# A fused attention and expert kernel: values and next scores of a tile issued together, in halves of one lasting PSUM pair

## The chip, the cores and the metric

The kernel runs on one core of a Trainium2 chip. The metric is the device time of one execution in microseconds (us). Before the change three runs took 1549.22, 1547.12 and 1549.45 us; their median is 1549.22 us. The engines are TensorE (PE, with its weight loads as PEld), VectorE (DVE), ScalarE (ACT), GpSimd (POOL) and the queue that issues the transfers (SP).

## The reference

The input is q, k and v for 8 batches of 8 heads, 576 positions and 64 channels. Attention is local: each chunk of 64 positions attends to itself only. Its output, as 4608 tokens of 512 channels, goes through four experts with a hidden width of 1024, and every token sums all four with normalised probabilities.

```python
scores = scale * np.matmul(q_c, k_c.transpose(0, 1, 2, 4, 3))   # chunks of 64
scores = scores - np.max(scores, axis=-1, keepdims=True)
attn = np.exp(scores)
attn = attn / (np.sum(attn, axis=-1, keepdims=True) + 1e-09)
out = np.matmul(attn, v_c)
...
p = domain_probs / (domain_probs.sum(-1, keepdims=True) + 1e-09)
for e in range(E):
    h = np.maximum(x @ w1[e], 0.0)
    out += p[:, e:e + 1] * (h @ w2[e])
```

## The kernel before

**Tiles and passes.** A tile is 128 tokens with all eight heads, so two chunks. Four tiles make a subset of 512 tokens, two subsets make a pair. The first subset is done plainly in eight passes over the experts' halves (0 to 7); then come four pairs of eight passes each. A product with float32 precision is made of three matmuls on a high and a low part (`hi` is a rounded copy by ACT, `lo` a subtraction by POOL or DVE). In the pairs the products go through a seven-product scheme for 2 by 2 blocks: `g` and `h` are the two column groups of the first layer (methods `p1` to `p7` of `Group`), `a` and `b` those of the second layer (`Outer`). Pair 0 holds sums and differences made in `first_pair_pass`, the later pairs run `later_pass`, where the second layer of one pass is woven with the first layer of the next by the list `WOVEN`, 28 products of six matmuls each. `first_later_pass` (list `FIRST`) starts that weave, `last_products` (list `ALONE`) ends it.

**Attention of a later tile.** The 32 tiles of the four pairs are prepared while earlier products run, one tile after the other: `a_scores` (16 matmuls of 64 by 64), `a_softmax` (maximum and subtraction on DVE, exponential on ACT), `a_weights` (sum, reciprocal and product on DVE), `a_transpose` (four PE transposes, and a copy by ACT), `a_values` (16 matmuls of 64 by 64, and a copy by ACT into `xraw`). All five use tiles of the PSUM pool `ps_a`, whose one buffer `psa` is a pair of banks: scores take it, transposes take it again, and values a third time. Between them stand products. For the tiles of pairs 0 and 1 the object `Beside` issues one step whenever its rate says so; for the tiles of pairs 2 and 3 the table `TILES` names for each pass which tile takes the places `EARLY` (4, 6, 9, 11) or `LATE` (13, 17, 21, 24) of the 28.

**PSUM and order.** Six further banks, A0 to C1, hold the products' results. The kernel is written with a manual schedule: each engine does its instructions in the order in which the functions issue them, and an instruction waits for those of other engines that used the same tile before it.

**Start and end.** `startup` fills PE with idle matmuls (`keep_warm`, 12, 14 and 3 of them) while the loads and the softmax of the first two tiles run. The idle matmuls write one bank of a `psa` pair, and the row sums of the first softmax (`start_weights`) stand in the other bank of that same pair. At the end `last_products` turns the last pair's result by PE transposes, tile by tile, and stores it.

**The joint of two pairs.** In the last pass of a pair the differences of the next pair's tokens (class `Tokens`, `t1` to `t4`) are made and split. The low part of `t4` is made by POOL in the next pair's first pass, between the splits of the hidden values (L268 in the trace).

Of the kernel before, what the change touches and what calls it, by code (L numbers as in the profile page):

```python
# [15 lines left out]
P = 128  # L16
C = 64
# [7 lines left out]
WAITS = {"loads": 12, "softmax": 14, "copy": 3}  # L25
# [5 lines left out]
def chunk_attention_moe(ctx: ExitStack, tc: tile.TileContext, qk, v, v0, dp, w1, w2, out):  # L31
# [64 lines left out]
    def transpose_probs():  # L96
        flat = by_e[0].rearrange("p e t -> p (e t)")
        for i in range(0, p_rows, P):
            n = min(P, p_rows - i)
            psa = bank()[:n, :P]  # L100
            rows = hpool.tile([P, P], F32, name="s3")[:n]
            nc.tensor.transpose(psa, flat[:, i : i + n], ident)
            nc.scalar.copy(out=rows, in_=psa)
            nc.sync.dma_start(out=p_t[i : i + n, :], in_=rows)
# [6 lines left out]
    xraw = {}  # L111

# [35 lines left out]
    def a_weights(t):  # L148

        s = st[t]  # L150
        s["e"] = att.tile([P, HG, 2, C], F32, name="e")
        z = s["psa"][:, 0, HG * C : HG * C + 2 * HG].rearrange("p (c j) -> p c j", c=2)
        a_norm(s["e"].rearrange("p j c k -> p c j k"), s["sc"], z)

    def a_transpose(t):
        s = st[t]
        ps = ps_a.tile([P, 2, 2 * HG * C], F32, name="psa")[:, 0].rearrange("p (j q) -> p j q", q=P)
# [39 lines left out]
    STEPS = (a_scores, a_softmax, a_weights, a_transpose, a_values)  # L197

    def attention(pair, together):
# [571 lines left out]
    def outputs(pair, i, g):  # L771

        psa = ps_a.tile([P, 2, 2 * HG * C], F32, name="psa")[:, 0].rearrange(
            "p (i m d) -> p i m d", i=2, d=P
        )
        for j in range(2):
            for m in range(2):
                output_part(pair, i + j, g + 2 * m, psa[:, j, m])
        stage = att.tile([P, 2, 2, P], F32, name=("e", "pt")[i // 2 % 2])
        nc.scalar.copy(out=stage, in_=psa)  # L780
# [71 lines left out]
    idle = ps_a.tile([P, 2, SUB], F32, name="psa")  # L852

    def keep_warm(n, cols=SUB):

        for _ in range(n):
            nc.tensor.matmul(
                idle[:, 0, :cols], lhsT=zeros[:, :P], rhs=zeros[:, :cols], start=True, stop=True
# [18 lines left out]
    def start_weights(t):  # L877
        es[t] = att.tile([P, 2 * HG, C], F32, name=("e", "pt")[t % 2])
        a_norm(es[t], sc[t], idle[:, 1, t * 2 * HG : (t + 1) * 2 * HG])

    def startup(beside):
# [11 lines left out]
        for f, k in QUADS[:2]:  # L893
# [48 lines left out]
    class Beside:  # L942


        def __init__(self, pair, n):
            self.steps = attention(pair, pair == 0) if pair < n_pairs else iter(())
            self.rate, self.due = len(STEPS) * PAIR * NT / n, 0.0

# [171 lines left out]
    EARLY, LATE = (4, 6, 9, 11), (13, 17, 21, 24)  # L1120
# [20 lines left out]
    def first_later_pass(n, *_):  # L1141
# [27 lines left out]
    def later_pass(n, ahead, late):  # L1169
# [13 lines left out]
        second_half(at, ahead[0], ahead[2:])  # L1183
# [15 lines left out]
        if n % 2 and more:  # L1199
            add(at, 5, lambda: probs_load(n + 1, 0))  # L1200
# [4 lines left out]
        late, x_low = [], []  # L1205
# [4 lines left out]
        if last_pass and more:  # L1210
# [18 lines left out]
        return (sc, left, *x_low), late  # L1229

    def second_half(at, sc, x_low=()):
# [6 lines left out]
        add(at, 4, *x_low, lambda: sc.sum("t4", 1, nc.gpsimd))  # L1238
        add(at, 6, lambda: sc.hi("t4", 1), lambda: sc.lo("t4", 1))

    def last_products(ahead):
# [4 lines left out]
        psa = []  # L1246

        def places(names):
            both = ps_a.tile([P, 2, 2 * HG * C], F32, name="psa")
            for t in (both[:, 0], both[:, 1], *(bank(name) for name in names)):  # L1250
                psa.append(t.rearrange("p (m d) -> p m d", d=P))

        def parts(i, *ms):
            for m in ms:
                output_part(pair, i, m, psa[(i + NT) % (2 * NT)][:, m])

        def store(i, eng):
# [88 lines left out]
```

## Time and profile before

| | |
|---|---|
| median of 3 runs | 1549.22 us (1547.12 to 1549.45) |
| the profiled execution's own time | 1546.54 us |
| its span | 1544.8 us |
| PE busy | 1524.5 us (99%) |
| PEld busy | 1239.6 us (80%) |
| DVE busy | 915.7 us (59%) |
| POOL busy | 888.5 us (58%) |
| ACT busy | 574.8 us (37%) |
| transfers | 314.16 MB, 203 GB/s on average |

The time of an execution holds the span and 1.7 us around it. PE is occupied in nearly the whole span, so a change is worth what it takes from, or adds to, the time between two of PE's products. In the tables of the profile a line number is that of the kernel before; L455 is the helper that issues all products, L139 the scores, L168 the values, L175 the copy of the values, L517 the copy of a running sum.

### The profile page before, as it was taken

To read this page: it belongs to the slowest core of one execution; us is meant where nothing else is said; L and a number is where in the kernel's file an instruction comes from. 1 tells how busy PE (TensorE), PEld (TensorE's weight loads), DVE (VectorE), ACT (ScalarE), POOL (GpSimd) and SP (SyncE) were. 2 spreads that over 40 slices of the span, in tenths; PEclk is the share of its full clock that TensorE was granted. 3 is DMA by queue.
4 is the path that set the end of the run, shared out by engine and by line. 5 is a ranking of instruction groups with operands and counts; after the bars stand their busy time and mean duration, and the time that the engine had idled before them with its cause. 6 is when DMAs were issued, how large, how long until landed. Compare 5 with 4: busy or idle time off the path is not lost.

```text
span 1544.8 us, 23430 instructions
## 1 busy us (share of the span) xinstructions
PE 1524.5 (99%) x8863; PEld 1239.6 (80%) x8863; DVE 915.7 (59%) x1284; ACT 574.8 (37%) x1000; POOL 888.5 (58%) x668
## 2 busy tenths in 40 slices
PE   8999999999999999999999999999999999999998
PEld 6878877888888887888888778888888788888886
DVE  4444454444443456677676855666767746666665
ACT  3343443444443434333333444333333343333332
POOL 2343577776666716555556855555557656555554
PEclk9999999999999999999999999999999999999999
DMA  5434348977676676666666667676666676666663
GB/s 193 123 122 148 101 134 278 312 248 226 234 245 205 208 268 205 200 224 215 208 207 198 201 211 227 200 226 208 223 189 198 189 234 198 200 201 203 201 191 135
DMA packets 164832, 314.16 MB, mean 203 GB/s; under 512 B 14177, under 2 KB 79985, under 8 KB 164721
## 3 DMA queue, kind: packets, MB, share of 16 engines
q1 hardware_dynamic: 164720, 312.68, 62.8%
q8 instruction: 70, 1.15, 0.3%
q14 instruction: 42, 0.34, 0.1%
HBM read 244.39 MB, written 68.23 MB: 202 GB/s over the span
## 4 chain that ended last, share of the span: by engine, by line
PE 78%; POOL 3%; DVE 2%; ACT 1%; issue 1%; DMA 0%; DVEq 0%; SPq 0%; POOLq 0%; ACTq 0%
PE A L455 41%; PE C L455 22%; PE B L455 12%; POOL hfl L637 2%; PE psa L168 1%; PE psa L139 1%; DVE xl L268 1%; PE psa L159 1%; PE psa L769 1%; DVE acc L683 1%; POOL wraw L628 0%; POOL xl L268 0%; DVE wraw L628 0%; ACT hfh L634 0%; ACT xh L265 0%
## 5 line engine op out<-in xcount | busy, mean ns | idle before, releaser
L637 POOL TENSOR_TENSOR hfl<-wraw,hfh 128x512 fp32r<-128x512 f32 x288 | 386.1, 1360 | 207.6 <-ACT hfh L634 205.7
L455 PE MATMUL A<-xh,wf 128*128 128x512 f32 (+1 forms) x1112 | 382.4, 390 | 3.9 <-ACT s L517 3.7
L455 PE MATMUL A<-hfh,wf 128*128 128x512 f32 x768 | 271.2, 394 | 1.6 <-DVE acc L683 1.0
L634 ACT CAST hfh<-wraw 128x512 fp32r<-128x512 f32 x288 | 174.2, 623 | 217.6 <-POOL wraw L628 57.5
L455 PEld LDWEIGHTS A<-xh,wf 128*128 128x128 f32 x1112 | 207.8, 188 | 49.8 <-ACT s L517 5.5
L517 ACT COPY s<-A 128x512 f32<-128x512 f32 x192 | 112.7, 587 | 347.2 <-PE A L455 343.0
L455 PE MATMUL A<-xl,wf 128*128 128x512 f32 (+1 forms) x556 | 214.8, 387 | 0.0
L455 PE MATMUL C<-xh,wf 128*128 128x512 f32 (+1 forms) x584 | 201.1, 391 | 0.0
L455 PEld LDWEIGHTS A<-hfh,wf 128*128 128x128 f32 x768 | 144.2, 188 | 33.1 <-DVE acc L683 2.5
L683 DVE TENSOR_TENSOR acc<-A,acc 128x512 f32<-128x512 f32 x174 | 119.3, 686 | 77.3 <-PE A L455 76.4
L455 PE MATMUL A<-hfl,wf 128*128 128x512 f32 x384 | 149.7, 390 | 0.0
L455 PE MATMUL C<-hfh,wf 128*128 128x512 f32 x384 | 135.4, 394 | 0.2
L268 POOL TENSOR_TENSOR hfl<-wraw,hfh 128x512 fp32r<-128x512 f32 x64 | 86.0, 1371 | 83.4 <-ACT hfh L265 79.8
L455 PEld LDWEIGHTS C<-xh,wf 128*128 128x128 f32 x584 | 109.1, 188 | 23.2
L455 PE MATMUL B<-xh,wf 128*128 128x512 f32 (+1 forms) x384 | 126.9, 383 | 0.0
L268 POOL TENSOR_TENSOR wf<-wraw,wf 128x512 fp32r<-128x512 f32 x70 | 91.4, 1331 | 55.9 <-ACT wf L265 53.6
L455 PEld LDWEIGHTS A<-xl,wf 128*128 128x128 f32 x556 | 104.3, 188 | 20.7
L628 POOL TENSOR_TENSOR wf<-wraw,wf 128x512 f32<-128x512 f32 x23 | 29.8, 1294 | 156.3 <-DVE wf L622 156.3
L455 PE MATMUL C<-xl,wf 128*128 128x512 f32 (+1 forms) x292 | 112.8, 388 | 0.0
L683 DVE TENSOR_TENSOR acc<-C,acc 128x512 f32<-128x512 f32 x90 | 62.1, 691 | 60.7 <-PE C L455 54.8
L637 POOL TENSOR_TENSOR hfl<-wf,hfh 128x512 fp32r<-128x512 f32 x48 | 71.2, 1483 | 35.5 <-ACT hfh L634 35.5
L455 PEld LDWEIGHTS C<-hfh,wf 128*128 128x128 f32 x384 | 72.1, 188 | 16.3 <-DVE acc L683 1.1
(175 smaller groups left out, 2735.5 us busy)
## 6 DMA issues: line engine op xcount, KB each, us to landing
wf<-w SPq DMA_DIRECT2D x336, 512.0 KB, 4.1
wraw<-in_w SPq DMA_DIRECT2D x128, 256.0 KB, 3.7
w<-wf SPq DMA_DIRECT2D x112, 256.0 KB, 4.4
qk_in<-in_qk SPq DMA_DIRECT2D x32, 512.0 KB, 4.7
v_in<-in_v SPq DMA_DIRECT2D x32, 256.0 KB, 4.8
w<-hfl SPq DMA_DIRECT2D x32, 256.0 KB, 2.4
w<-hfh SPq DMA_DIRECT2D x32, 256.0 KB, 2.6
w<-hfh SPq DMA_DIRECT2D x48, 128.0 KB, 2.5
```

Of the source, the lines that this page charges most:

```text
L139: nc.tensor.matmul(s["sc"][half, c, j], lhsT=s["x"][rows, g, 0, h], rhs=s["x"][rows, g, 1, h], start=True, stop=True,)
L159: nc.tensor.transpose(ps[:, j], s["e"][:, j].rearrange("p c k -> p (c k)"), ident)
L168: nc.tensor.matmul(av[half, c, j], lhsT=s["v"][rows, 2 * j + odd], rhs=s["pt"][rows, j, half], start=True, stop=True,)
L268: eng.tensor_tensor(out=t[1], in0=src, in1=t[0].bitcast(F32), op=ALU.subtract)
L455: nc.tensor.matmul(out, lhsT=lhs(k, a), rhs=rhs(k, b), start=first and i == 0, stop=last and i == len(parts) - 1, skip_group_check=not (fi ...
L517: nc.scalar.copy(out=t, in_=self.a)
L628: (eng or nc.vector).tensor_tensor(out=self.values[place, k], in0=self.values[a, k], in1=self.values[b, k], op=op)
L634: nc.scalar.copy(out=self.part(name, 0)[:, k], in_=self.values[name, k])
L637: (eng or nc.gpsimd).tensor_tensor(out=self.part(name, 1)[:, k], in0=self.values[name, k], in1=self.part(name, 0)[:, k].bitcast(F32), op=A ...
L683: nc.vector.tensor_tensor(out=acc[key], in0=src, in1=acc[key], op=ALU.add)
L769: nc.tensor.transpose(out_ps, acc[pair + 1, m + NK * s][:, j * P : (j + 1) * P], ident)
```

## The change

1. **One lasting pair.** `psa` is allocated once, and no longer per step. Scores use the first half of the columns of both its banks (`blocks(0)`), values the second half (`blocks(1)`). Transposes still take one whole bank.
2. **Joint steps.** `a_next(t, after)` issues the values of tile t with their copy and, right behind, the scores of the next tile, with the loads for it. The maximum and exponential come one place later. `EARLY` and `LATE` become three places each; for `Beside` a tile has four yields and `rest`, an empty one for pair 0.
3. **Startup.** 10 idle matmuls in place of the first 12; they write bank C1, and the row sums stay in `psa`. The third split of the first weights stands ahead of the first transpose, values of tile 0 ahead of the transposes of tile 1, scores of tile 2 behind these.
4. **Joints of pairs and of stages.** The low part of `t4` goes from POOL to DVE, that of `b22` three places later. In `first_later_pass` the two groups change their banks (index 1 - g), and the split of `t1` and the sum `t4` move behind the split of `b21`. One of the loads of probabilities moves from place 5 to place 13.
5. **Last outputs.** A unit is now one 128-channel plane of four tiles (`plane`): four transposes, one copy (ACT or DVE; the last one is divided between both), one store with rows of 512 bytes. Two planes stand behind b2, five behind a4, one behind b4; before it were two tiles behind b2, four halves and two tiles behind a4, and four halves behind b4.

```diff
-WAITS = {"loads": 12, "softmax": 14, "copy": 3}
+WAITS = {"loads": 10, "softmax": 14, "copy": 3}
...
+    psa = ps_a.tile([P, 2, 2 * HG * C], F32, name="psa")
...
-    def halves(ps):
-
-        return ps[:, :, : HG * C].rearrange("p c (j k) -> p c j k", k=C)
+    def blocks(i):
+
+        return psa[:, :, i * HG * C : (i + 1) * HG * C].rearrange("p c (j k) -> p c j k", k=C)
 
     def a_scores(t):
         s = st[t]
-        s["psa"] = ps_a.tile([P, 2, 2 * HG * C], F32, name="psa")
-        s["sc"] = halves(s["psa"])
+        s["sc"] = blocks(0)
...
-        av = halves(ps_a.tile([P, 2, 2 * HG * C], F32, name="psa"))
+        av = blocks(1)
...
         a_load(first)
+        yield
+        a_next(None, first)
         for t in range(first, last):
-            for step in STEPS:
-                if not (together and step is a_softmax):
-                    yield
-                if together and step is a_transpose:
-                    yield
-                step(t)
-                if step is a_scores:
-                    a_load_v(t)
-                    if t + 1 < last:
-                        a_load(t + 1)
+            for step in (a_softmax, a_weights, *(rest * [None]), a_transpose):
+                yield
+                if step:
+                    step(t)
+            yield
+            a_next(t, t + 1 if t + 1 < last else None)
+
+    def a_next(t, after):
+
+        if t is not None:
+            a_values(t)
+        if after is not None:
+            a_scores(after)
+            a_load_v(after)
+            if (after + 1 - NT) % (PAIR * NT):
+                a_load(after + 1)
...
-            self.names = (*((f"A{g}", f"B{g}", f"C{g}") if apart else ("A0", "B0", "C0")), f"B{g if apart else 0}", "s2")
+            i = 1 - g if apart else 0
+            self.names = (f"A{i}", f"B{i}", f"C{i}", f"B{i}", "s2")
...
-    idle = ps_a.tile([P, 2, SUB], F32, name="psa")
+    idle = bank("C1")
...
-        a_norm(es[t], sc[t], idle[:, 1, t * 2 * HG : (t + 1) * 2 * HG])
+        a_norm(es[t], sc[t], psa[:, 1, t * 2 * HG : (t + 1) * 2 * HG])
...
-        for f, k in QUADS[:2]:
+        for f, k in QUADS[:3]:
             w1_split(f, k, nc.gpsimd)
         start_transpose(0)
         keep_warm(WAITS["copy"])
         start_weights(1)
-        for f, k in QUADS[2:]:
-            w1_split(f, k, nc.gpsimd)
-        start_transpose(1)
         start_values(0)
         start_x(0)
+        start_transpose(1)
+        start_scores(2)
+        w1_split(1, 1, nc.gpsimd)
         start_values(1)
         start_x(1)
-        start_scores(2)
         start_scores(3)
...
-    EARLY, LATE = (4, 6, 9, 11), (13, 17, 21, 24)
+    EARLY, LATE = (6, 9, 11), (17, 21, 24)
...
-        add(at, places[0], lambda: a_scores(t), lambda: a_softmax(t), lambda: a_load_v(t))
-        if i + 1 < PAIR * NT:
-            add(at, places[0], lambda: a_load(t + 1))
-        for place, step in zip(places[1:], STEPS[2:]):
-            add(at, place, lambda step=step: step(t))
+        after = t + 1 if i + 1 < PAIR * NT else None
+        if i == 0:
+            add(at, 13, lambda: a_next(None, t))
+            add(at, 14, lambda: a_softmax(t))
+        add(at, places[0], lambda: a_weights(t))
+        add(at, places[1], lambda: a_transpose(t))
+        add(at, places[2], lambda: a_next(t, after))
+        if after:
+            add(at, places[2] + 1, lambda: a_softmax(after))
...
         put(12, "b22", 1)
-        put(12, "t1", 0)
-        add(at, 12, lambda: sc.sum("t4", 0, nc.gpsimd))
         put(13, "b21", 1)
+        put(13, "t1", 0)
         put(13, "t3", 0)
+        add(at, 13, lambda: sc.sum("t4", 0, nc.gpsimd))
...
-            add(at, 5, lambda: probs_load(n + 1, 0))
+            add(at, 13, lambda: probs_load(n + 1, 0))
...
-            x_low = [lambda: x.lo("t4", nc.gpsimd)]
             late = [
-                (0, lambda: x.hi("b22")), (0, lambda: first_load(pair + 2)), (5, lambda: x.lo("b22")),
+                (0, lambda: x.hi("b22")), (0, lambda: first_load(pair + 2)), (5, lambda: x.lo("t4")),
+                (8, lambda: x.lo("b22")),
             ]
...
+        def plane(s, m, ps, engs):
+
+            ps = ps.rearrange("p (i d) -> p i d", d=P)
+            for j in range(NT):
+                output_part(pair, s * NT + j, m, ps[:, j])
+            pool, name, bufs = stages.pop()
+            stage = pool.tile([P, NT, P], F32, name=name, bufs=bufs)
+            for k, eng in enumerate(engs):
+                part = slice(k * NT // len(engs), (k + 1) * NT // len(engs))
+                eng(out=stage[:, part], in_=ps[:, part])
+            t = (1 + pair * PAIR + s) * NT
+            nc.sync.dma_start(
+                out=out[t * P : (t + NT) * P, m * P : (m + 1) * P].rearrange("(i p) d -> p i d", p=P),
+                in_=stage,
+            )
...
             if name == "b2":
-                places(("C1", "C0"))
-                parts(4, *range(NK))
-                parts(5, *range(NK))
+                plane(1, 0, bank("C1"), act)
+                plane(1, 1, bank("C0"), act)
             elif name == "a4":
...
+                plane(1, 2, psa[:, 0], act)
+                plane(1, 3, bank("B1"), dve)
+                plane(0, 0, bank("B0"), act)
+                plane(0, 1, bank("C1"), dve)
+                plane(0, 2, bank("C0"), act)
...
+        plane(0, 3, bank("A1"), act + dve)
```

**How the instructions move.** On PE, in a later pass, around the values of a tile (`psa<-pt,v_in`) and the scores (`psa<-qk_in`); names of product banks begin with A, B or C, and a row names in brackets the engines or transfers whose count its first matmul waits for. Before, scores of this tile, a product, and much later its values:

```order
L139 MATMUL psa<-qk_in 64x64 [waits DMAHW2_49,PE_49]
L139 MATMUL psa<-qk_in 64x64 x15
L455 MATMUL C_7051<-hfh_6898,wf_6876 128x512 [waits DMAHW7_49]
...
L168 MATMUL psa<-pt,v_in 64x64 [waits DMAHW6_49,Activation_49]
L168 MATMUL psa<-pt,v_in 64x64 x15
L455 MATMUL C_7059<-xh_5522,wf_7008 128x512 [waits DMAHW5_49,DVE_49]
```

The same place in the changed kernel:

```order
L462 MATMUL A_6939<-xh_5519,wf_6923 128x512
L169 MATMUL psa<-pt,v_in 64x64 [waits DMAHW1_49,Activation_49]
L169 MATMUL psa<-pt,v_in 64x64 x15
L140 MATMUL psa<-qk_in 64x64 [waits DMAHW2_49,Activation_49]
L140 MATMUL psa<-qk_in 64x64 x15
L462 MATMUL C_6997<-xh_5473,wf_6971 128x512 [waits DMAHW7_49,DVE_49]
```

The scores of the next tile stand directly behind the values; both rows have a wait for a count of ACT. On ACT the rows of such a place in the changed kernel are these (`pt` is the copy of the transposes, `xraw` that of the values, the row behind it the exponential of the next scores):

```order
L524 COPY s_7397<-A_7299 128x512 [waits PE_49,Activation_49]
L162 COPY pt<-psa 128x512 [waits DVE_49,PE_49]
L176 COPY xraw<-psa 128x2x4x64 [waits PE_49]
L188 ACTIVATE psa<-psa 128x2x256 [waits DVE_49,PE_49,Activation_49]
```

In the program the values wait for the count that the copy into `pt` reaches, and in each of the 28 joints the scores wait for the count that the copy into `xraw` reaches, the copy of the values just ahead of them; before, one or more products stood between that copy and the next scores.

On POOL, at the joint of two pairs, before:

```order
L637 TENSOR_TENSOR hfl_8375<-wf_8252,hfh_8373 128x512 [waits Activation_49]
L268 TENSOR_TENSOR xl_8438<-xraw,xh_8437 128x1024 [waits PE_49]
L628 TENSOR_TENSOR wraw<-wraw 128x512
L637 TENSOR_TENSOR hfl_8480<-wraw,hfh_8478 128x512 [waits Activation_49]
```

and in the changed kernel:

```order
L644 TENSOR_TENSOR hfl_8302<-wf_8178,hfh_8300 128x512 [waits Activation_49]
L635 TENSOR_TENSOR wraw<-wraw 128x512
L644 TENSOR_TENSOR hfl_8407<-wraw,hfh_8405 128x512 [waits Activation_49]
```

The row of 1024 elements (`xl`, the low part of `t4`) has left POOL; it stands on DVE, ahead of the low part of `b22`.

More of the change, by code (lines that the diff above doesn't have):

```diff
@@ L99, in transpose_probs @@
             n = min(P, p_rows - i)
-            psa = bank()[:n, :P]
+            ps = bank()[:n, :P]
             rows = hpool.tile([P, P], F32, name="s3")[:n]
-            nc.tensor.transpose(psa, flat[:, i : i + n], ident)
-            nc.scalar.copy(out=rows, in_=psa)
+            nc.tensor.transpose(ps, flat[:, i : i + n], ident)
+            nc.scalar.copy(out=rows, in_=ps)
             nc.sync.dma_start(out=p_t[i : i + n, :], in_=rows)
@@ L151, in a_weights @@
         s["e"] = att.tile([P, HG, 2, C], F32, name="e")
-        z = s["psa"][:, 0, HG * C : HG * C + 2 * HG].rearrange("p (c j) -> p c j", c=2)
+        z = psa[:, 0, HG * C : HG * C + 2 * HG].rearrange("p (c j) -> p c j", c=2)
         a_norm(s["e"].rearrange("p j c k -> p c j k"), s["sc"], z)
@@ L156, in a_transpose @@
         s = st[t]
-        ps = ps_a.tile([P, 2, 2 * HG * C], F32, name="psa")[:, 0].rearrange("p (j q) -> p j q", q=P)
+        ps = psa[:, 0].rearrange("p (j q) -> p j q", q=P)
         for j in range(HG):
@@ L195, in a_norm, with attention @@
         nc.vector.tensor_tensor(out=e, in0=a, in1=r, op=ALU.mult)
-    STEPS = (a_scores, a_softmax, a_weights, a_transpose, a_values)
-    def attention(pair, together):
+    def attention(pair, rest):
         first = (1 + pair * PAIR) * NT
@@ L771, in outputs @@
     def outputs(pair, i, g):
-        psa = ps_a.tile([P, 2, 2 * HG * C], F32, name="psa")[:, 0].rearrange(
-            "p (i m d) -> p i m d", i=2, d=P
-        )
+        ps = psa[:, 0].rearrange("p (i m d) -> p i m d", i=2, d=P)
         for j in range(2):
             for m in range(2):
-                output_part(pair, i + j, g + 2 * m, psa[:, j, m])
+                output_part(pair, i + j, g + 2 * m, ps[:, j, m])
         stage = att.tile([P, 2, 2, P], F32, name=("e", "pt")[i // 2 % 2])
-        nc.scalar.copy(out=stage, in_=psa)
+        nc.scalar.copy(out=stage, in_=ps)
         t = (1 + pair * PAIR) * NT + i
@@ L857, in keep_warm @@
             nc.tensor.matmul(
-                idle[:, 0, :cols], lhsT=zeros[:, :P], rhs=zeros[:, :cols], start=True, stop=True
+                idle[:, :cols], lhsT=zeros[:, :P], rhs=zeros[:, :cols], start=True, stop=True
             )
@@ L942, in chunk_attention_moe, with __init__ @@
     class Beside:
-        def __init__(self, pair, n):
-            self.steps = attention(pair, pair == 0) if pair < n_pairs else iter(())
-            self.rate, self.due = len(STEPS) * PAIR * NT / n, 0.0
+        def __init__(self, pair, n, rest):
+            self.steps = attention(pair, rest)
+            self.rate, self.due = ((4 + rest) * PAIR * NT + 1) / n, 0.5
         def load(self):
@@ L1182, in later_pass @@
             add(at, i, f)
-        second_half(at, ahead[0], ahead[2:])
+        second_half(at, ahead[0])
         add(at, 12, lambda: sc.sum("t3", 0, nc.gpsimd))
@@ L1204, in later_pass @@
                 attend(at, pair + 1, places, i)
-        late, x_low = [], []
+        late = []
         if first_pass and pair > 1:
@@ L1228, in later_pass, with second_half @@
                 f()
-        return (sc, left, *x_low), late
-    def second_half(at, sc, x_low=()):
+        return (sc, left), late
+    def second_half(at, sc):
         add(at, 0, lambda: sc.sum("t2", 1))
@@ L1237, in second_half @@
         add(at, 4, lambda: sc.hi("t3", 1), lambda: sc.lo("t3", 1))
-        add(at, 4, *x_low, lambda: sc.sum("t4", 1, nc.gpsimd))
+        add(at, 4, lambda: sc.sum("t4", 1, nc.gpsimd))
         add(at, 6, lambda: sc.hi("t4", 1), lambda: sc.lo("t4", 1))
@@ L1245, in last_products @@
         steps = {"ab"[g]: Outer(g, n_run - 1, ahead[1], ahead[0], True) for g in range(2)}
[L1246 to L1257, printed above, removed]
-            name, k = (("s1", 0), ("s2", 0), ("s3", 0), ("wraw", 0), ("wraw", 0), ("wraw", 0), ("e", 0), ("pt", 0))[i]
-            pool = {"e": att, "pt": att, "wraw": wpool}.get(name, hpool)
-            stage = pool.tile([P, SUB], F32, name=name, bufs=N_RAW if name == "wraw" else 1)
-            eng(out=stage, in_=psa[(i + NT) % (2 * NT)].rearrange("p m d -> p (m d)"))
-            t = (1 + pair * PAIR) * NT + i
-            nc.sync.dma_start(out=out[t * P : (t + 1) * P, :], in_=stage)
+        stages = [(hpool, f"s{i}", 1) for i in (1, 2, 3)]
+        stages += [(wpool, "wraw", N_RAW)] * 3 + [(att, "e", 1), (att, "pt", 1)]
+        def plane(s, m, ps, engs):
[12 more added lines that the diff above has]
+            )
+        act, dve = [nc.scalar.copy], [nc.vector.tensor_copy]
         for i, name in enumerate(ALONE):
@@ L1269, in last_products @@
             if name == "b2":
[L1270 to L1272 removed]
+                plane(1, 0, bank("C1"), act)
+                plane(1, 1, bank("C0"), act)
             elif name == "a4":
[L1274 to L1285 removed]
+                plane(1, 2, psa[:, 0], act)
[4 more added lines that the diff above has]
+        plane(0, 3, bank("A1"), act + dve)
     with tc.manual_schedule():
[L1288 removed]
+        beside = [Beside(0, (n_pass - 3) * 2 * NK, 1), Beside(1, (n_pass - 1) * 26 - 4, 0)]
         startup(beside[0])
```

13 lines of the change are left out of this document (removed).

## The prediction

> **What bounds the kernel now.** I read the totals of the page first, then its chain of waits.
>
> ```profile
> span 1544.8 us, 23430 instructions
> PE 1524.5 (99%) x8863; PEld 1239.6 (80%) x8863; DVE 915.7 (59%) x1284; ACT 574.8 (37%) x1000; POOL 888.5 (58%) x668
> PE 78%; POOL 3%; DVE 2%; ACT 1%; issue 1%; DMA 0%; DVEq 0%; SPq 0%; POOLq 0%; ACTq 0%
> ```
>
> PE is occupied in 1524.5 of 1544.8 us, so all that PE ever stands idle is 20.3 us. No transfer appears in the chain. Each part of the change is therefore worth what it takes from, or adds to, the time from one product's start to the next. What PE does in a joint was read from its timeline; L455 is a product, L139 scores, L168 values, L175 their copy.
>
> ```profile
> 1099.55 0.69 PE L168 MATMUL psa<-pt,v_in 64*64 64x64 f32 x32
> 1100.31 0.59 ACT L175 COPY xraw<-psa 128x512 f32<-128x512 f32 x1 [2.73 <-PE psa L168]
> ...
> 1102.80 0.39 PE L455 MATMUL A<-hfh,wf 128*128 128x512 f32 x1
> ...
> 1103.12 0.69 PE L139 MATMUL psa<-qk_in 64*64 64x64 f32 x32
> ...
> 1103.74 0.50 PE L455 MATMUL A<-xh,wf 128*128 128x512 f32 x1
> ...
> 1105.24 0.39 PE L455 MATMUL B<-xh,wf 128*128 128x512 f32 x1
> ...
> 1106.60 0.39 PE L455 MATMUL A<-hfh,wf 128*128 128x512 f32 x1
> ```
>
> A product's six matmuls take 1106.60 - 1105.24 = 1.36 us, 0.23 each. A step set between products costs more than its own streaming: 0.32 from the last product's start to the step's (1103.12 - 1102.80), 0.62 until the next product, less the 0.23 that would pass anyway, and 0.14 because the six matmuls behind it take 1.50 (1105.24 - 1103.74). That is 0.85 per step, 1.71 for values and scores apart.
>
> **Joint steps.** One of the two entries is saved, if the scores follow the values at once. They don't, I think. Both are halves of one tile and of the same two banks, the program orders accesses by tile and not by column, and in the changed program the first score matmul of each of the 28 joints waits for the count that the copy of the values just ahead reaches. The profile of before shows that sharing a pair is enough to wait:
>
> ```profile
> 8.90 3.19 PE L857 MATMUL psa<-s 128*128 128x512 bf16 x14
> ...
> 12.21 0.70 DVE L190 TENSOR_REDUCE psa<-A 128x8 f32<-128x512 f32 x1 [1.65 <-PE psa L857]
> ...
>   ACT xraw L175: 0.4, 1
> ```
>
> The row sums go to one bank of the pair and waited 1.65 us for idle matmuls that fill the other; the last row, from the view of the scores' line, shows one score that stood behind a copy of values already. The Trainium skill ("PSUM — Partial Sum Buffer", section on bank collisions) asks for the same: PSUM is to be guarded by bank and quadrant and not by address, because TensorE writing columns of a bank while another engine reads other columns of it is an error. Under it the scores cannot overtake the copy in halves of a bank; without it the joint would be the first rival below.
>
> The price: the copy ends 1100.31 + 0.59 - 1099.55 = 1.35 us after the values' start. PE restarts about 0.05 after a copy that it awaits (890.73 + 0.58 = 891.31 against 891.36, quoted further down). The joint then takes 0.32 + 1.35 + 0.05 + 0.62 - 0.23 + 0.14 = 2.25, against 1.71: **+0.54, times 28 = +15.2 us**. Behind the waiting score matmul stand all products; nothing else can run on PE.
>
> ACT works in order, and a copy that finds a cast ahead of it ends later:
>
> ```profile
> 706.99 0.69 PE L168 MATMUL psa<-pt,v_in 64*64 64x64 f32 x32
> ...
> 707.09 1.34 ACT L634 CAST hfh<-wraw 128x512 fp32r<-128x512 f32 x2 [0.25 <-PE B L455]
> ...
> 708.34 0.58 ACT L175 COPY xraw<-psa 128x512 f32<-128x512 f32 x1
> ...
>   PE psa L168: 48.1, 18
> ```
>
> Here it ends at 708.92, 1.93 after the values' start, 0.58 later than above. Today nobody waits for that; in a joint PE does. This is the place of a `LATE` tile, and I give 0.58 to each of the six joints at such places: 3.5. The last row, from the view of L175, says that 18 of the 32 copies began on PE's release, so 14 did not; eight of those lie outside `LATE`. I take five of them at 0.58, 2.9. Bounds: none of the late ones (0), or the six at 0.58 and the eight at twice that, as casts also await transfers there (3.5 + 9.3 = 12.8). **Joints: 15.2 + 6.4 = +21.6 us, between +15.2 and +28.0.**
>
> The maximum and exponential one place later, and three places for four, cost nothing: from scores to transposes lie two or more products of 1.36 us and more, DVE is busy 59% and ACT 37%. The loads for the next tile move along with the scores on SP, whose transfers appear nowhere in the chain; the load of probabilities, moved eight places, likewise.
>
> **Joints of pairs.** The low part of `t4` leaves POOL.
>
> ```profile
> 884.37 2.31 DVE L268 TENSOR_TENSOR xl<-xraw,xh 128x1024 fp32r<-128x1024 f32 x1
> ...
> 885.53 3.40 POOL L268 TENSOR_TENSOR xl<-xraw,xh 128x1024 fp32r<-128x1024 f32 x1
> ...
> 888.89 1.28 POOL L628 TENSOR_TENSOR wraw<-wraw 128x512 f32<-128x512 f32 x1
> ...
> 889.50 0.39 PE L455 MATMUL A<-hfh,wf 128*128 128x512 f32 x1
> 890.20 0.62 ACT L634 CAST hfh<-wraw 128x512 fp32r<-128x512 f32 x1 [6.62 <-POOL wraw L628]
> 890.73 0.58 ACT L517 COPY s<-A 128x512 f32<-128x512 f32 x1
> ...
> 891.36 0.50 PE L455 MATMUL A<-xh,wf 128*128 128x512 f32 x1 [1.47 <-ACT s L517]
> ...
> 1221.04 0.50 PE L455 MATMUL A<-xh,wf 128*128 128x512 f32 x1 [1.45 <-ACT s L517]
> ```
>
> POOL's 3.40 us hold the sum, the sum holds ACT's cast, the cast holds the copy of A for which PE stands: 891.36 - 889.50 - 0.23 = 1.63 us. Without it the sum can begin 3.4 earlier and the whole stall goes. On DVE the operation takes 2.31 (row 884.37), and `b22`'s, which stood there, goes three places on, so DVE's load at this place stays. Two such joints: **-3.3 us**; bounds 0 (DVE's sums come late in turn) and -3.8 (with the slow restart of 0.11 and more each).
>
> **First later pass.** PE stands twice where the banks of one group are taken again:
>
> ```profile
> 587.08 0.50 PE L455 MATMUL A<-hfh,wf 128*128 128x512 f32 x1 [0.61 <-DVE wraw L622]
> ...
> 590.48 1.72 POOL L637 TENSOR_TENSOR hfl<-wraw,hfh 128x512 fp32r<-128x512 f32 x1
> ...
> 592.25 0.50 PE L455 MATMUL B<-hfl,wf 128*128 128x512 f32 x1 [1.24 <-POOL hfl L637]
> ```
>
> The exchange of banks takes the first wait away (0.6). The second is POOL's work, and POOL stays back to back there; with the first wait gone PE arrives earlier at it, or at the split of `t1` that is now POOL's later. **-0.9 us**, between 0 and -1.9 plus restarts, -3.
>
> **Startup.** Up to the first products PE's work hangs on DVE's softmax of the first tiles; the row sums' wait is quoted above (12.21).
>
> ```profile
> 17.64 1.09 PE L826 MATMUL B<-ident,pt 128*128 128x128 f32 x4 [2.13 <-DVE pt L195]
> 18.66 1.97 PE L839 MATMUL B<-s,qk_in 64*64 64x64 f32 x32
> 20.42 1.15 PE L839 MATMUL A<-s,qk_in 64*64 64x64 f32 x32
> ...
> 22.84 0.68 DVE L182 TENSOR_REDUCE m<-C 128x8 f32<-128x512 f32 x1
> 23.36 1.21 PE L455 MATMUL B<-xh,wf 128*128 128x256 f32 x8
> ...
> 28.07 0.66 PE L826 MATMUL B<-ident,e 128*128 128x128 f32 x4
> ...
> 10.00:20.00 10.00, 5.74 (x47) 3.52 (x46) 4.11 (x9) 3.83 (x7) 4.97 (x4) 0.86 0.89 314
> ...
> PEld A L815 <- DMA xraw<-in_qk: 0.2, 1, 0.2
> ```
>
> With the idle matmuls in their own bank the row sums lose the 1.65 above, and the second ones a like wait behind the three idle matmuls (estimated as 1.5, since the sums run one behind the other and shift together). In the 10 to 20 us window the granted clock is 0.86, and groups of one kind show it: transposes 1.09 against 0.66 later, values 1.97 against 1.15. If PE gets there earlier, 0.43 + 0.82 of that may go. Together 4.4; but the next softmax's maximum (22.84) needs DVE, which still splits the first tokens, and I give back 0.7: **-3.7 us**, from -1.65 (the first wait alone) to -4.4. Two idle matmuls fewer at the very start bring nothing: of the waits up to 9 us the last row says that the second tile's scores stood for their load after all twelve, and would stand for it longer. Moving the third split of weights costs nothing: POOL does the four in the same order, and is idle 42% of the time.
>
> **Last outputs.**
>
> ```profile
> 1537.40 0.69 DVE L683 TENSOR_TENSOR acc<-A,acc 128x512 f32<-128x512 f32 x1 [2.44 <-PE A L455]
> ...
> 1538.52 0.59 ACT L1261 COPY s<-psa 128x512 f32<-128x512 f32 x1 [2.73 <-PE psa L769]
> ...
> 1540.31 0.68 DVE L1261 COPY wraw<-B 128x512 f32<-128x512 f32 x1
> ...
> 1541.32 0.40 SPq L1263 DMA_DIRECT2D out<-wraw  x1
> ```
>
> After the last sum (ends 1538.09) come four copies and four stores; the last is issued 3.2 us later and lands at the span's end, 3.5 us on. With one plane, behind the sum come 0.43 until a copy could begin (1538.52 - 1538.09), an estimated 0.3 more for four transposes in place of one, 0.4 for half a copy (0.59 undivided, and a part that doesn't shrink), and 0.33 from the last copy's end to the issue (1541.32 - 1540.99): 1.5, so 1.7 sooner, plus up to 0.2 for transfers that no longer queue. Four more transposes ahead of b4 cost some 0.4 (four take 0.66 at 28.07, the last one's drain within). **-1.5 us**, from 0 (rows of 512 bytes land later) to -2.5.
>
> **Sum.** +21.6 - 3.3 - 0.9 - 3.7 - 1.5 = +12.2, on the profiled execution's 1546.54: 1558.7. That execution lies 2.7 below the median of the runs, 1549.22, so for the median 1561.
>
> **Rivals.**
> *The scores don't wait* (the wait is for an older copy, or one that is done). PE then streams 32 more matmuls in one group, 0.69 - 0.22 = 0.47, and a joint takes 0.85 + 0.47 = 1.32 against 1.71: -0.39 times 28 = -10.9. With the other gains -20.3, so 1529. It decides once the pause in a joint is under 0.39 + 9.4/28, some 0.7 us beyond streaming, where the wait is worth 0.93. For it speaks that the columns are disjoint; against it the row sums' 1.65. Chance 6%.
> *The gains eat the loss.* The copies are all on time (+15.2) and startup, pair joints and tail bring their bounds (-4.4 - 3.8 - 3 - 2.5 = -13.7): +1.5, 1551. For it speaks that ACT is idle 63% of the time; against it that 14 copies were late. Chance 10%.
> *ACT blocks.* ACT takes casts that await a transfer or POOL, in order, and the copy stands behind them while PE, standing, makes nothing that would release them: two more us in six joints, +12, so 1573. For it speaks the chance of casts of weights next to the copies in pairs 0 and 1; against it that transfers are no part of the chain. Chance 8%.
> The forecast holds the remaining 76%.
>
> **How the numbers follow.** A measurement of this kernel tells about 0.2%, 3.1 us, from no change. From the sum's bounds: 15.2 - 13.7 to 28.0 - 2 about the median is 1551 to 1575, both corners unlikely together; the range is 1551 to 1570. Faster: the first rival and a little of the second, 8%. Within 0.2%: half of the second and some of the forecast's edge, 7%. Slower: 85%.
>
> **What would show it.** In the changed profile PE's scores should carry an idle time put down to ACT's `xraw` copy, about 28 times near 0.9 us, and PE's busy share should fall. The stalls of 1.47 and 1.45 should be gone, the first product of 256 columns should stand near 19.5, and one copied plane near the end. If the scores start right behind the values, my central step is wrong, and the time is under 1535; if the idle times at joints reach 2 us and more, ACT's order is to blame.

## The result, and the profile after

The changed kernel took 1561.35 us (median of 6 runs, 1559.73 to 1562.41) against 1548.33 us for the kernel before on the same chips (6 runs, 1545.49 to 1549.45): a ratio of 1.0086, 95% interval 1.0073 to 1.0099. It is slower, by 13 us; the forecast was 1561 us, in a range of 1551 to 1570.

The totals of the changed kernel, and the three longest groups of PE's waits, who waited for whom: us in total, times, the longest.

```profile
span 1557.9 us, 23373 instructions
PE 1518.0 (97%) x8861; PEld 1241.3 (80%) x8861; DVE 917.6 (59%) x1287; ACT 572.5 (37%) x1000; POOL 886.2 (57%) x666
...
PE psa L140 <- ACT xraw L176: 25.8, 28, 1.6
PE A L821 <- DMA xraw<-in_qk: 1.7, 1, 1.7
PE C L462 <- POOL hfl L644: 1.5, 2, 1.3
```

PE is busy 6.5 us less than before (1524.5), and the span is 13.1 us longer. One group of waits stands out: the scores (L140 in the changed kernel) behind the copy of the values (L176), once in each of the 28 joints, 25.8 us in all. In a timeline the first two numbers of a row are its start and its length, and brackets hold the idle time before it and who ended it. The first of the two timelines is a joint in which ACT was free, the second one at a `LATE` place.

```profile
1073.35 0.69 PE L169 MATMUL psa<-pt,v_in 64*64 64x64 f32 x32
...
1074.12 0.59 ACT L176 COPY xraw<-psa 128x512 f32<-128x512 f32 x1 [2.79 <-PE psa L169]
...
1074.75 0.69 PE L140 MATMUL psa<-qk_in 64*64 64x64 f32 x32 [0.70 <-ACT xraw L176]
...
1075.38 0.50 PE L462 MATMUL C<-xh,wf 128*128 128x512 f32 x1
```

```profile
716.15 0.69 PE L169 MATMUL psa<-pt,v_in 64*64 64x64 f32 x32
...
716.26 1.34 ACT L641 CAST hfh<-wraw 128x512 fp32r<-128x512 f32 x2 [0.25 <-PE B L462]
...
717.51 0.58 ACT L176 COPY xraw<-psa 128x512 f32<-128x512 f32 x1
...
718.14 0.69 PE L140 MATMUL psa<-qk_in 64*64 64x64 f32 x32 [1.29 <-ACT xraw L176]
```

The scores start 0.04 to 0.05 us after the copy ends (1074.71 and 718.09): 1.40 us after the values' start in the one, 1.99 in the other. No score overtakes a copy, though they use other columns.

### The profile page after: what moved, and what is told of

It is laid out like the page before. It is cut to its first block, busy times and chain, and to the rows that moved or that the text cites. A ratio compares the mean times of both kernels' runs of the same rounds, so it can differ in the third digit from the quotient of the medians.

```text
span 1557.9 us, 23373 instructions
## 1 busy us (share of the span) xinstructions
PE 1518.0 (97%) x8861; PEld 1241.3 (80%) x8861; DVE 917.6 (59%) x1287; ACT 572.5 (37%) x1000; POOL 886.2 (57%) x666
## 4 chain that ended last, share of the span: by engine, by line
PE 89%; DVE 4%; ACT 2%; POOL 2%; DMA 2%; issue 1%; SPq 0%; POOLq 0%; DVEq 0%; ACTq 0%
PE A L462 44%; PE C L462 26%; PE B L462 14%; PE psa L140 1%; ACT xraw L176 1%; PE psa L169 1%; PE psa L160 1%; DVE xl L275 1%; DVE wraw L635 1%; DVE acc L691 1%; ACT hfh L641 1%; POOL wf L275 0%; PE psa L777 0%; DMA w<-wf 0%; DVE wraw L629 0%
## 5 line engine op out<-in xcount | busy, mean ns | idle before, releaser
L462 PE MATMUL A<-xh,wf 128*128 128x512 f32 (+1 forms) x1112 | 380.7, 389 | 1.0 <-ACT s L524 0.7
L462 PE MATMUL A<-hfh,wf 128*128 128x512 f32 x768 | 271.2, 394 | 1.0 <-DVE acc L691 1.0
L462 PEld LDWEIGHTS A<-xh,wf 128*128 128x128 f32 x1112 | 207.8, 188 | 45.6 <-ACT s L524 1.7
L462 PE MATMUL A<-xl,wf 128*128 128x512 f32 (+1 forms) x556 | 214.7, 387 | 0.0
L462 PE MATMUL C<-xh,wf 128*128 128x512 f32 (+1 forms) x584 | 201.0, 391 | 0.0
L462 PEld LDWEIGHTS A<-hfh,wf 128*128 128x128 f32 x768 | 144.2, 188 | 32.4 <-DVE acc L691 2.5
L462 PE MATMUL A<-hfl,wf 128*128 128x512 f32 x384 | 149.7, 390 | 0.0
L462 PE MATMUL C<-hfh,wf 128*128 128x512 f32 x384 | 134.2, 391 | 0.2
L462 PEld LDWEIGHTS C<-xh,wf 128*128 128x128 f32 x584 | 109.1, 188 | 23.0
L462 PE MATMUL B<-xh,wf 128*128 128x512 f32 (+1 forms) x384 | 126.0, 382 | 0.0
L462 PEld LDWEIGHTS A<-xl,wf 128*128 128x128 f32 x556 | 104.3, 188 | 21.1
L462 PE MATMUL C<-xl,wf 128*128 128x512 f32 (+1 forms) x292 | 112.8, 388 | 0.0
L462 PEld LDWEIGHTS C<-hfh,wf 128*128 128x128 f32 x384 | 72.1, 188 | 15.9 <-DVE acc L691 1.1
```

What stands on the lines that cost most here:

```text
L462: nc.tensor.matmul(out, lhsT=lhs(k, a), rhs=rhs(k, b), start=first and i == 0, stop=last and i == len(parts) - 1, skip_group_check=not (fi ...
```

## The experiments

All runs stand beside runs of the kernel before on the same chip; "before" is its median there. Kernels are compared with each other by their ratios to it. Line numbers are each kernel's own: runs made from the changed kernel have products at L462 to L465 and scores at L140, those made from the kernel before at L455 and L139, apart from the joints alone (L462, L140).

**Scores first.** In the joint, the two groups change places:

```diff
     def a_next(t, after):
+        if after is not None:
+            a_scores(after)
         if t is not None:
             a_values(t)
         if after is not None:
-            a_scores(after)
             a_load_v(after)
```

> The changed kernel with one edit: in the 28 joints the next tile's scores are issued first and the values behind them, so that no score stands behind the copy of the values. Theory (the pause is the wait for that copy): the 28 pauses of 25.8 us in total vanish, a joint takes 0.32 + 0.47 + 0.62 - 0.23 + 0.14 = 1.32 us beyond the regular pace instead of the 2.25 to 3.1 measured (69.8 us over all 28), so 28 x 1.32 = 37.0 and the time falls by 32.8 us to about 1528.5. Rival A (a group of 64 small matmuls, or the turn from values to scores, is slow by itself): the pause stays, 1561. Rival B (PE gets ahead, and waits for DVE or ACT on the same pair of banks elsewhere): between 1535 and 1555, with new waits at transposes or values.

Measured: 1526.64 us against 1547.71, ratio 0.9865 (0.9852 to 0.9879), so 2.2% or 34 us under the changed kernel. A joint of it by PE's timeline:

```profile
716.93 0.39 PE L463 MATMUL A<-xh,wf 128*128 128x512 f32 x1
717.25 0.69 PE L140 MATMUL psa<-qk_in 64*64 64x64 f32 x32
717.77 0.65 PE L169 MATMUL psa<-pt,v_in 64*64 64x64 f32 x32
718.34 0.50 PE L463 MATMUL C<-xh,wf 128*128 128x512 f32 x1
```

From product to product it takes 1.41 us, in 27 of the 28 joints; less the regular 0.23 and with 0.14 for the restart it is 1.32, the price that I had written for a joint without the wait. Over all 28 joints the start times of PE's matmuls give 37.0 us beyond the regular pace in this kernel, 69.2 in the changed one, and 47.7 for 56 separate steps (0.852 each, from the 64 of before). So the idea of a shared entry is worth its 10.7 us, and the wait took 32.2 back. Rival A falls: values and scores in one group cost nothing by themselves. Rival B too: no wait at values or transposes took its place. This kernel is faster than both.

**The joint undone.** Values at their place, the scores of the next tile one product later; the lasting pair and all else as changed.

```diff
-        add(at, places[2], lambda: a_next(t, after))
+        add(at, places[2], lambda: a_values(t))
         if after:
-            add(at, places[2] + 1, lambda: a_softmax(after))
+            add(at, places[2] + 1, lambda: a_next(None, after))
+            add(at, places[2] + 2, lambda: a_softmax(after))
```

(For pairs 0 and 1 a yield parts the two steps in the same way.)

> The changed kernel with the joint undone: values at the joint's place, scores of the next tile one product or step later, the maximum behind these; the lasting pair and the other three parts stay. Theory: each of the 28 joints (69.8 us in all) becomes two separate steps at 0.857 us (48.0), so the time falls by 21.8 to about 1539.6, which is 8.7 us under the kernel before, the worth of startup, joints of pairs, first later pass and last outputs together. Rival A of the run with scores first: the same. Rival (the other parts are worth nothing): 1548.

Measured: 1538.11 against 1547.71, ratio 0.9938 (0.9925 to 0.9950). The time lies 23 us under the changed kernel by the ratios, and 9.6 under the kernel before: the other parts together do gain what they were priced at.

**The joints alone.** The kernel before with the lasting pair and the joint steps, and with startup, joints of pairs, first later pass and last outputs as before:

```diff
+    psa = ps_a.tile([P, 2, 2 * HG * C], F32, name="psa")
...
-    idle = ps_a.tile([P, 2, SUB], F32, name="psa")
+    idle = lasting = psa
...
+            a_next(t, t + 1 if t + 1 < last else None)
...
-    EARLY, LATE = (4, 6, 9, 11), (13, 17, 21, 24)
+    EARLY, LATE = (6, 9, 11), (17, 21, 24)
```

> The kernel before with the joint steps and the lasting pair alone; startup, joints of pairs, first later pass and last outputs as before. Theory: the joints cost the same 21.8 us here, so 1548.3 + 21.8 = about 1570. Rival (part of the loss comes from the other parts, or the joints cost more only because those shift the work): under 1565.

Measured: 1569.38 against 1547.71, ratio 1.0143 (1.0129 to 1.0157), +21.7 us. The loss belongs to the joints and needs no other part. The view of its scores' line counts PE and its weight loads together, hence 56 for 28 joints, and gives what the changed kernel's gives (55.4, 56):

```profile
  ACT xraw L176: 55.3, 56
```

**The copy ahead of the casts.** In the woven passes the joint is issued ahead of the splits of its place, so ACT finds no cast before the copy:

```diff
-        add(at, places[2], lambda: a_next(t, after))
+        at.setdefault(places[2], []).insert(0, lambda: a_next(t, after))
```

> The changed kernel with one edit: where a place of the woven lists has splits and the joint, the joint (with its copy on ACT) is issued ahead of the splits, so no cast stands ahead of the copy at the places 24. Theory (ACT works in order): the seven pauses of about 1.5 us become 0.92, so 7 x 0.59 = 4.1 us less, about 1557.2, less if the casts that now come later hold PE. Rival (those copies are late for another reason): 1561.

Measured: 1556.59 against 1547.71, ratio 1.0056 (1.0042 to 1.0070). Its wait at the scores:

```profile
PE psa L140 <- ACT xraw L176: 22.2, 28, 1.6
```

That is 3.6 us less than 25.8, or 0.6 for each of the six joints at the places 24 (I had written seven into the expectation; there are three per pair, in two pairs). All six now take 2.34 us from product to product like those where ACT is free, where they took 2.93 to 2.98. The ratios differ by 0.3%, 4.6 us, with an uncertainty of about 3. ACT's place in its queue set the length of these waits. What is left at 1.6 are joints of pair 0, where other casts stand ahead.

**The copy done twice.** The changed kernel, with a second copy of the same values behind the first:

```diff
-        nc.scalar.copy(
-            out=xraw[pair][:, :, i * P : (i + 1) * P].rearrange("p j (c q) -> p c j q", c=2), in_=av
-        )
+        for _ in range(2):
+            nc.scalar.copy(
+                out=xraw[pair][:, :, i * P : (i + 1) * P].rearrange("p j (c q) -> p c j q", c=2), in_=av
+            )
```

> The changed kernel with the copy of the values done twice on ACT, the second behind the first; the next scores wait for the second. Theory (the pause is the copy's time, taken from ACT): each of the 28 joints grows by one copy, 0.53 to 0.62 us, so 15 to 17 us more, about 1577, and the short pauses go from 0.92 to about 1.5. Rival (the copy is hidden in part behind some other end of the pause): less than 10 us more.

Measured: 1586.06 against 1547.19, ratio 1.0244 (1.0230 to 1.0258), 24 us over the changed kernel where 15 to 17 were expected.

```profile
PE psa L140 <- ACT xraw L177: 43.0, 28, 2.2
```

The wait grew by 17.2 us, 0.61 for each joint: one more copy, as expected, and nothing of it is hidden. The other 7 us are not in the wait. They stand behind it, in PE's timeline at one of the long pauses, and in the windows there (the numbers behind POOL's are the granted clock, the transfers' share and GB/s):

```profile
729.15 0.69 PE L169 MATMUL psa<-pt,v_in 64*64 64x64 f32 x32
731.75 0.69 PE L140 MATMUL psa<-qk_in 64*64 64x64 f32 x32 [1.91 <-ACT xraw L177]
732.38 0.60 PE L463 MATMUL A<-hfh,wf 128*128 128x512 f32 x1
732.77 0.63 PE L463 MATMUL A<-hfl,wf 128*128 128x512 f32 x1
733.20 1.06 PE L463 MATMUL A<-hfh,wf 128*128 128x512 f32 x2
...
724.00:729.00 5.00, 5.00 (x25) 3.96 (x23) 1.78 (x4) 2.31 (x4) 3.33 (x3) 1.00 0.50 172
729.00:734.00 5.00, 3.09 (x69) 2.42 (x69) 1.51 (x3) 2.31 (x5) 3.73 (x3) 0.86 0.65 185
734.00:739.00 5.00, 5.00 (x19) 4.05 (x18) 3.18 (x5) 1.13 (x2) 0.51 (x1) 0.80 0.61 204
```

Behind the pause matmuls start 0.43 us apart (732.77 to 733.20) in place of 0.23, and the granted clock is 0.86 and 0.80. After the startup 40 matmuls of products in this trace last over 0.6 us, in the changed kernel's none: 40 x 0.2 = 8 us. They stand behind six of the ten joints whose pause was 1.9 us or more, and behind none of the eighteen of 1.54. (A pause is counted here and in the last section as the idle time in the row's brackets plus 0.22 us, which is what such a joint takes beyond the 1.41 of one with scores first.) So the expectation was right on the wait, and left out a second price that a longer wait brings.

**Startup alone, and its idle bank alone.** The kernel before with the third part of the change; then with nothing but the idle matmuls' own bank:

```diff
-    idle = ps_a.tile([P, 2, SUB], F32, name="psa")
+    idle = bank("C1")
+    sums = ps_a.tile([P, 2, SUB], F32, name="psa")
...
-        a_norm(es[t], sc[t], idle[:, 1, t * 2 * HG : (t + 1) * 2 * HG])
+        a_norm(es[t], sc[t], sums[:, 1, t * 2 * HG : (t + 1) * 2 * HG])
```

> The kernel before with the startup alone (10 idle matmuls, their own bank, the order of the first tiles). My step said -3.7 us, between -1.65 and -4.4; the changed kernel's profile gave -2.9 by the 37th product, with a load that landed late, and the runs with scores first, apart and copy first gave -4.9, -4.5 and -3.3. Theory (the row sums' wait and the slow clock): about 4 under the kernel before, and 15 to 20 us into the span no window with a clock near 0.86. Rival (the second tile's load sets the end of startup, so nothing is gained on average): within 1 us.

> The kernel before with one edit: the idle matmuls of the startup write bank C1, and the row sums have the pair for themselves; number and order of the startup's work as before. Theory (sharing a pair is enough to wait): the waits of 1.65 and 1.53 us at the row sums are gone from the profile, and the time falls by 1.65 to 3.2, by more if the slow clock near 15 us goes with them. Rival (the gain of 5.1 us that the startup alone gave comes from the order of the first tiles): no change within 1 us. Where the time lies between both, the rest is the order's.

Measured: 1541.86 against 1546.93, ratio 0.9968 (0.9955 to 0.9980), -5.1 us, for the whole startup; 1542.97 against 1547.19, ratio 0.9972 (0.9962 to 0.9982), -4.2 us, for the bank alone. The waits of the row sums before, and then DVE and the clock in the profile of the bank alone (start, length; the window's clock is behind POOL's numbers):

```profile
DVE psa L190 <- PE psa L857: 3.2, 2, 1.6
```

```profile
9.81 0.70 DVE L184 TENSOR_TENSOR A<-A,m 128x512 f32<-128x512 f32 x1
10.41 0.69 DVE L190 TENSOR_REDUCE psa<-A 128x8 f32<-128x512 f32 x1
...
11.59 0.69 DVE L195 TENSOR_TENSOR e<-A,z 128x512 f32<-128x512 f32 x1
12.20 0.69 DVE L190 TENSOR_REDUCE psa<-A 128x8 f32<-128x512 f32 x1
...
10.00:20.00 10.00, 7.76 (x143) 5.51 (x140) 6.54 (x13) 5.37 (x10) 5.00 (x4) 1.00 1.05 362
```

Both row sums follow DVE's work with no wait, where the two waited 3.2 us in all, and the clock is 1.00 in place of 0.86; it is 1.00 in the profile of the whole startup too. One changed bank for matmuls whose result nobody reads is worth most of the startup's gain; the order of the first tiles adds at most about 1 us, which the intervals don't tell from nothing.

**Joints of pairs and first later pass alone; last outputs alone.** The kernel before with the fourth part, and with the fifth:

```diff
-            x_low = [lambda: x.lo("t4", nc.gpsimd)]
...
+                (5, lambda: x.lo("t4")), (8, lambda: x.lo("b22")),
```

> The kernel before with the fourth part alone (low part of t4 on DVE, that of b22 later, banks exchanged in the first later pass, one load moved). Theory: the two stalls of 1.63 go (-3.3) and the first later pass gives -0.75 as in the changed kernel's profile, together -4.0. In the profiles of scores first and copy first one of the two stalls came back as 1.4 us before a DVE L630 operation, with DVE's low part at 2.35 instead of 1.21 us beside a POOL operation; if that is common, -2.6.

```diff
-        for i in range(NT):
-            parts(i, 2, 3)
-            store(i, (nc.scalar.copy, nc.vector.tensor_copy)[i % 2])
+        plane(0, 3, bank("A1"), act + dve)
```

> The kernel before with the last outputs alone. Theory: -1.5 us, from the last product to the end 6.0 instead of 7.8 with 0.4 more for transposes ahead. Rival (the stores with rows of 512 bytes land so much later that the end stays): 0.

Measured: 1543.58 and 1545.51, both against 1546.93; ratios 0.9978 (0.9969 to 0.9987) and 0.9991 (0.9982 to 1.0000), -3.4 and -1.4 us. The second is at the edge of what can be told from nothing; its profile shows it: the end stands 6.00 us after the start of the last product's last matmul in place of 7.80, and that product starts 0.43 us later behind the added transposes. Startup, pairs and outputs alone sum to -9.9; the run with the joint undone, which has all three, gave -9.6.

**The low parts later.** Scores first, with the two splits on DVE moved on, since the run with scores first had one stall of 1.4 us left at the second joint of pairs:

```diff
-                (5, lambda: x.lo("t4")), (8, lambda: x.lo("b22")),
+                (7, lambda: x.lo("t4")), (9, lambda: x.lo("b22")),
```

> Scores first, and at the joints of pairs the low parts of t4 and b22 behind the products 7 and 9 instead of 5 and 8, behind the sums for which PE stands there. Theory (DVE's low part, slow beside POOL, holds the sum that frees PE's bank): both stalls of 0.25 and 1.4 us at 862 and 1187 go, 1 to 2 us less than 1526.6. Rival (something else holds the bank): the same stalls, or the stall goes to the product that reads t4.

Measured: 1527.40 against 1546.93, ratio 0.9877 (0.9863 to 0.9890): no gain over scores first (0.9865). The stall of 1.4 us is absent from this profile, as it is from most (the last section counts them), and another stands in both joints:

```profile
878.95 0.50 PE L463 MATMUL C<-xl,wf 128*128 128x512 f32 x1 [0.43 <-DVE xl L276]
...
1204.85 0.50 PE L463 MATMUL C<-xl,wf 128*128 128x512 f32 x1 [0.43 <-DVE xl L276]
```

The rival was right: the stall went to a product that reads a low part. My theory had also taken the wrong operation for the cause. What held PE in the run with scores first was the low part of `t3`, which no version moves (the last section shows it).

## Why the prediction was right, point by point

The sizes, from the profile after by the start times of PE's matmuls, and from the run of each part by itself:

| term | forecast | profile after | part alone |
|---|---|---|---|
| joints, copy on time and late | +15.2 + 6.4 = +21.6 | 69.2 - 47.7 = +21.5 | +21.7 |
| joints of pairs | -3.3 | -3.2 | -3.4 with the next |
| first later pass | -0.9 | -0.7 | |
| startup | -3.7 | -2.8 | -5.1 |
| last outputs | -1.5 | -1.4 | -1.4 |
| sum | +12.2 | +13.3; the span grew by 13.1 | +11.8 |

That the median came within 0.4 us of the forecast is in part luck. The startup was sized too small by 1.4 us, and the median of before that the forecast was built on (1549.22) lies 0.9 above the one that the changed kernel was measured against (1548.33).

**Joint steps.** The central step held: one tile in the same banks means one order, and 28 waits, of which the shortest add 0.93 us to a joint. Seventeen joints take 2.34 us from product to product, as worked out; six at `LATE` places 2.93 to 2.98 (+0.59 to 0.64, forecast 0.58). In pairs 0 and 1 two take 0.87 more, two 0.35 and one 0.07, together 2.5 where five of 0.58 were allowed; the total fits, the single sizes don't. The rival that scores don't wait is refuted for this program, but its price was right to a few tenths of a microsecond, as scores first shows. Sharing the tile is enough for the wait: the row sums of before waited for idle matmuls that fill the other bank of the pair, and no longer do where the two have a tile each (the run with the idle bank alone). No run gave scores and values a tile and banks each. Nor did one try whether the chip itself would let scores and the copy run in halves of a bank. The rule of the Trainium skill quoted in the prediction ("PSUM — Partial Sum Buffer", bank collisions) forbids it; no run here shows an error, only that the program keeps to the rule.

**Joints of pairs.** In the changed kernel the products that stood for 1.47 and 1.45 us start without it; PE's two stalls of 1.63 became 0.0 each, and the products behind have moved up by 1.63 and 1.61 us.

**First later pass.** The step was right that the first wait goes and the second stays, at another product and behind POOL as before:

```profile
603.00 0.50 PE L462 MATMUL C<-hfl,wf 128*128 128x512 f32 x1 [1.26 <-POOL hfl L644]
```

**Startup.** The mechanism was right: a wait for the pair, and a slow clock that it brings about. One profile was not enough to size it. In the profiled run the second tile's load came late and the clock was not quite full, which hid a part:

```profile
8.03 1.24 PE L821 MATMUL A<-xraw 64*64 64x64 f32 x20 [1.69 <-DMA xraw<-in_qk]
...
10.00:20.00 10.00, 9.97 (x156) 6.84 (x155) 5.97 (x12) 4.99 (x9) 4.99 (x4) 0.92 0.91 317
...
19.61 1.22 PE L462 MATMUL B<-xh,wf 128*128 128x256 f32 x8
...
25.24 0.65 PE L832 MATMUL B<-ident,e 128*128 128x128 f32 x4 [1.06 <-DVE hfl L470]
```

Here the first product stands at 19.61, near the 19.5 of the prediction and 3.75 sooner than before (23.36); the wait of 1.06 at 25.24 then takes 0.9 of it back. The 121st matmul of the products, the first of 512 columns, starts at 44.19, 45.63, 44.23 and 45.05 us in the four profiles with the startup of before, and at 41.35, 39.27, 39.68, 40.89, 40.76, 39.26 and 40.63 in the seven with the new one: 44.8 against 40.3 on the mean, so -4.5. That is just outside the range of -1.65 to -4.4, as is the -5.1 of the part alone: the term was sized too small. Single profiles with one startup lie up to 2 us apart there, so one pair of them sizes it poorly.

**Last outputs.** The time from the last sum to the end fell by 1.8 us, and 0.4 came back for the transposes ahead. The halves of the last copy did not run side by side as I had assumed:

```profile
1552.36 0.69 DVE L691 TENSOR_TENSOR acc<-A,acc 128x512 f32<-128x512 f32 x1 [1.14 <-PE A L462]
...
1553.80 0.37 ACT L1267 COPY s<-A 128x256 f32<-128x256 f32 x1 [2.25 <-PE A L777]
1554.21 0.42 DVE L1267 COPY s<-A 128x256 f32<-128x256 f32 x1 [1.15 <-ACT s L1267]
```

DVE's half waits for ACT's. Both read halves of one bank and write halves of one tile; which of the two makes the wait wasn't tried.

## What to carry to other kernels

In this program two pieces of work in halves of one PSUM tile are one piece: whatever is issued second waits for the other engines that already work on the first. Before two groups are joined to save an entry, look at what each leaves behind; the one whose result must be copied out belongs last, where its copy runs beside other work. Here that order alone turned +0.9% into -1.4%.

## What was not expected of the hardware

**A pause of PE can cost more than its length.** The run with the copy done twice shows it: pauses of 0.93 to 1.54 us left no trace in the clock, while six of the ten of 1.9 to 2.4 us were followed by matmuls 0.43 us apart. In the run with the copy first one of two pauses of 1.79 us did the same, with seven slow matmuls; in the changed kernel and in the joints alone neither of the two did.

Where a pause falls decides. The clock in the traces is 0.50 in stretches of 3.41 us, and within a trace these begin whole multiples of 3.41 us apart. Two such stretches and the next one each, in the run with the copy done twice, around the joint quoted above and around one whose pause of 2.4 us was not hit (the first numbers are the length and PE's busy time, the granted clock is the third from the end):

```profile
729.22:732.63 3.41, 1.50 (x66) 1.30 (x66) 1.29 (x3) 2.31 (x4) 3.41 (x3) 1.00 0.73 229
732.63:736.05 3.42, 3.42 (x9) 2.67 (x9) 0.90 (x2) 0.00 (x0) 0.18 (x1) 0.50 0.55 158
...
166.02:169.43 3.41, 1.84 (x37) 1.59 (x38) 0.11 (x1) 1.49 (x3) 2.47 (x2) 1.00 0.72 230
169.43:172.85 3.42, 3.42 (x16) 2.82 (x16) 0.94 (x2) 0.60 (x1) 0.00 (x0) 1.00 0.34 103
```

PE stood idle for 1.91 us of the first stretch and the next ran at half the clock; the other pause began before its stretch did and left 1.57 in it. So it is throughout the twelve traces, cut in this way between the startup and the last microseconds: all six stretches with 1.67 us or more of idle PE were followed by one at 0.50, one of the five with 1.57 was, and none with less. The Trainium skill ("TensorE: Matmul & The Clock Gate", Part 1) tells of a clock at full or half rate, halved after an idle window of about 3.4 us that runs freely of the kernel. The pitch of 0.43 against 0.23 and the stretches of 3.41 us agree with it; but a stretch that was idle for about half its length sufficed here. Most of the matmuls in the rest of it were the small ones of 64 by 64, and whether these count less than products is open.

**A subtraction on DVE takes 1.21 or 2.35 us in the same place.** It is the low part of `t3`, at the second joint of pairs, with POOL at work beside it; first the changed kernel, then the run with scores first, and PE's stall there:

```profile
1218.07 4.39 POOL L644 TENSOR_TENSOR hfl<-wraw,hfh 128x512 fp32r<-128x512 f32 x2 [0.17 <-ACT hfh L641]
...
1220.10 1.21 DVE L275 TENSOR_TENSOR xl<-xraw,xh 128x1024 fp32r<-128x1024 f32 x1
```

```profile
1183.76 3.31 POOL L645 TENSOR_TENSOR hfl<-wraw,hfh 128x512 fp32r<-128x512 f32 x2 [0.16 <-ACT hfh L642]
...
1185.80 2.35 DVE L276 TENSOR_TENSOR xl<-xraw,xh 128x1024 fp32r<-128x1024 f32 x1
...
1188.81 0.50 PE L463 MATMUL A<-xh,wf 128*128 128x512 f32 x1 [1.21 <-DVE wraw L630]
```

DVE starts 2.03 us after POOL in the one and 2.04 in the other, at the start of POOL's second operation (1220.09 and 1185.79). In the one POOL's two operations take 1.08 us longer, in the other DVE's takes 1.14 longer, and then PE stands. In the run with the low parts later DVE's operation of this size takes 1.21 (at 877.68) with no POOL operation beside it. So in each case one of the two ran as if alone, and the other lost nearly the time that this one took (1.21, and 1.27 for POOL's second operation). Of the seven profiles that have the fourth part, two show this stall, this one and that with the copy first. The Trainium skill ("GPSIMD Engine Reference", section 1, Specifications) says that POOL shares its SBUF interfaces with DVE and contends with DVE operations that have two inputs in SBUF; the operations here are of that kind and the trace agrees with it. What decides who yields is open; the order of the starts was the same in both.
